# At most three of the late weight transfers on their way at a time

## The chip, the cores and the metric

The kernel runs on one core of one Trainium2 chip. The metric is the device time in microseconds (us) of one execution; the time of a kernel is the median of several. Five engines work side by side, each on its own queue of instructions: PE (TensorE, matrix products and transposes), DVE (VectorE), ACT (ScalarE), POOL (GpSimd) and SP (SyncE). SP computes nothing here. It issues nearly all DMA transfers, strictly in the order of its queue: an issue that has to wait holds up all issues behind it. A transfer's end is seen through a semaphore, and "landing" means the moment at which that semaphore says that all of its data are in place.

## The reference

Two layers stand one behind the other. First comes block-sparse attention over 4 batches, 8 heads, 768 positions and a head dimension of 64. Blocks of 32 positions attend to their neighbours, to the first and last block, and to three sampled blocks; the first and the last block attend to everything.

```
scores = scale * np.matmul(q, k.transpose(0, 1, 3, 2))
...
scores = np.where(mask, scores, -1000000000.0)
...
return np.matmul(attn, v).astype(np.float32)
```

Its output, 3072 rows of 512, is the input x of a soft mixture of experts with 8 experts and 4 slots each:

```
logits = x @ phi
d = softmax of logits over the 3072 rows;  slot_input = d.T @ x
h = np.maximum(slot_input[e] @ w1[e], 0.0);  slot_out[e] = h @ w2[e]
c = softmax of logits over the 32 slots;  out = c @ slot_out
```

Everything is in 32-bit floating point. The two weights w1 and w2 are 8 x 512 x 1024 and 8 x 1024 x 512, 33.6 MB in all, over half of the bytes that the kernel moves.

## The kernel before

**Stages.** The attention runs batch by batch over pairs of blocks. For each pair PE computes scores (`s`, L516), DVE and ACT make exponentials of them (L533, L538), DVE transposes them (L545), and PE multiplies them with the values (`av`, L610). POOL copies the three sampled blocks' values into staging tiles `vrs` (L461). Finished tiles of x are transposed (`mxt`, L803), turned into logits (`ml`) and summed into the slots' input (`ms`). After the last tile a short chain of small steps gives the slots' input `sT`. Then the feed-forward runs: sixteen steps `ffn1` (`pf`, L1227) with w1, sixteen steps `ffn2` (`pso`, L1235) with w2, eight for each half (`s_` = 0, 1) of the output's columns. The results of a half are combined with the softmax c (`po`, L1331), copied out (`ob`) and stored (L1288 to L1296).

**Weights.** The weights are cut into NW = 64 tiles of 128 x 1024 numbers, 512 KB each, used in the order of their numbers, two for each step. All loads go through `load_w` (L205, issue in L211) and `load_wk` (L230) onto SP's queue. There isn't room for all of them at once:

- Tiles 0 to 10 (pool `wpre`), 11 to 13 (`ktile`), 14 to 19 (`v0`) and 20 to 22 (`ptd`) are loaded during the attention, in pieces of 32 rows and 128 KB. The last three groups take the place of keys, values and probabilities that are no longer needed.
- Tiles 23 to 25 go into the second buffer of the keys as soon as it is free (the `("ktile", "k", 12, 13)` entry of L1038), each in two pieces of 512 columns, 256 KB. In the trace they are called `kw`.
- Tiles 26 to 43 are the late ones (`load_late`, L1180, called in L1210 to L1214): twelve go where the attention's staging tiles were (`w`), six into the values' second buffer (`v`), each again in two pieces of 256 KB, in the order of LORD (L59), in which a negative number means one of the six.
- Tiles 44 to 63 are loaded whole, 512 KB each, each when `done_w` (L1216) and `next_w` (L1193) find that an earlier tile's place has been used up.

**What sets the order.** Up to L1147 a planner (class `Plan`) lists all steps with costs and due times in a model of its own and emits them in that order; the pieces of tiles 0 to 22 are also paced (`pace`): each waits for a product that the planner expects to be done by then (L176 to L180), and their model keeps a rate. The pieces of tiles 23 to 25 belong to the plan too, without pacing. From L1153 on, the loads are emitted as the program writes them; what they wait for is that their place is free, and for the DMA semaphore that they share with an earlier transfer. The planner also emits small fill products on PE where it expects it to wait (`warm`, `st` in L376).

Of the kernel before, what the change touches and what calls it, by code (L numbers as in the profile page):

```python
# [21 lines left out]
P = 128  # L22
# [34 lines left out]


LORD = [0, 1, 2, 3, 4, 5, -1, -2, -3, -4, 6, 7, 8, 9, -5, -6, 10, 11]  # L59
LCOLS = [slice(c, c + LC) for c in range(0, WP, LC)]  # L60
H1, HALF = 3, 4
CPES = [0, 0, 3, 3, 3, 2, 0, 0]
# [14 lines left out]
class Plan:  # L77
# [6 lines left out]
    def add(self, f, opts, deps, key, acq=(), byte=0, pre=None, pace=False):  # L84
        t = Task(f, opts if isinstance(opts, list) else [opts], deps, key, acq, byte, pre, pace)
        self.tasks.append(t)
        return t
# [96 lines left out]
def attn_moe_kernel(ctx, tc, qT, kT, vfull, vtab, sampled, phi, w1, w2, out):  # L184
    nc = tc.nc
    PE, ACT, DVE, POOL, SP = nc.tensor, nc.scalar, nc.vector, nc.gpsimd, nc.sync
# [18 lines left out]
    def load_w(m, pool, t=None, rows=slice(0, P), cols=slice(0, WP)):  # L205
        if wtile[m] is None and t is None:
            t = pool.tile([P, WP], F32, name=f"w{m}", tag="w")
        elif t is None:
            t = wtile[m].rearrange("p c f -> p (c f)")
        n, j = m // PW, m % PW  # L210
        i = SP.dma_start(out=t[rows, cols], in_=wsrc[n].rearrange("p c f -> p (c f)")[rows, j * WP + cols.start:j * WP + cols.stop])  # L211
        wtile[m] = t.rearrange("p (c f) -> p c f", f=512 if n < 2 * NE else CW)
        return i

    wk = {}

    def new_wk(tag):
        k = KW[tag]
        if tag == "ktile":
            wk[tag] = pk.tile([P, k, WP], F32, name="kw", tag=tag)  # L220
        else:
            buf = ptdb if tag == "ptd" else vbuf[int(tag[1])]
            if tag == LATEW[1]:

                o = [VH * (j % 2) + WP * (j // 2) for j in range(k)]
                wk[tag] = [buf[:, c:c + WP] for c in o]
            else:
                wk[tag] = buf[:, 0:k * WP].rearrange("p (k f) -> p k f", k=k)

    def load_wk(m, tag, j, rows=slice(0, P), cols=slice(0, WP)):  # L230

        return load_w(m + j, None, wk[tag][j] if tag == LATEW[1] else wk[tag][:, j, :], rows, cols)
# [127 lines left out]
    add = plan.add  # L360
# [675 lines left out]
    m, n = NPRE, first[B - 1]  # L1036
    t_last = state.t_acc
    for tag, pool, n0, n1 in (("ktile", "k", 3, 5), ("v0", "v", 5, 10), ("ptd", "ptd", 5, 8), ("ktile", "k", 12, 13)):  # L1038
        go = lambda j: [qks[min(N - 1, n + n0 + (n1 - n0) * j // KW[tag])]]
        a_w = add(lambda t, tag=tag: new_wk(tag), ("NONE", 0.0), go(0), N + m, acq=[(pool, [t_last])])  # L1040
        for j in range(KW[tag]):
            parts = [(slice(r, r + LR), slice(0, WP)) for r in range(0, P, LR)]
            if n0 == 12:
                parts = [(slice(0, P), c) for c in LCOLS]
            for i, (r, c) in enumerate(parts):
                add(lambda t, m=m, tag=tag, j=j, r=r, c=c: load_wk(m, tag, j, r, c), ("SP", 0.47), go(j) + [a_w],
                    N + m + j + i / 4, byte=4 * WP * P // len(parts), pace=n0 < 12)
        m += KW[tag]

# [118 lines left out]
    wpool = [wpre] * NPRE  # L1168
# [11 lines left out]
    def load_late(pool, j=None):  # L1180

        m = len(wpool)
        for c in LCOLS:
            if j is None:
                load_w(m, pool, None, slice(0, P), c)
            else:
                load_wk(m - j, pool.tag, j, slice(0, P), c)
        wpool.append(pool)

    for tag in EARLYW:  # L1190
# [14 lines left out]
    load_group(LATEW[0], False)  # L1205

    new_wk(LATEW[1])
    lw, vw = [Place(lwb, f"w{n}") for n in range(NLB)], Group(LATEW[1])
    lw += [Place(pw, f"ptt{(nt[0] + r) % PTB}") for r in (2, 3)]
    for n in LORD:  # L1210
        if n < 0:
            load_late(vw, -1 - n)
        else:
            load_late(lw[n])  # L1214
# [214 lines left out]
```

## Time and profile before

| | |
|---|---|
| time, median of 3 | 316.43 us (315.21 to 322.23) |
| the profiled execution's own time | 316.63 us |
| its span, first to last instruction | 314.6 us |
| mean granted clock of TensorE in it | 0.984 |
| DMA packets, bytes | 34658, 63.62 MB |
| HBM read, written | 56.19 MB, 6.29 MB |

Groups of instructions in the profile have the line of the kernel, the engine, the operation, then what is written and read by the program's names (`av<-v,ptt`), shapes, and a count. PEld is the weight load of TensorE, which overlaps PE. A row of the chain of waits has the start, the length and the step, with what it is or what it waited for; "issue" is time in which an engine waited for nothing that the profile shows. A row of the timeline has the start, the length, the engine (SPq: issue on SP's queue), the line, the operation, the names and the count. A row of the DMA issues has the names, the queue, the count, the KB of each and the median time from issue to landing. A row of stretches has the stretch, its length, each engine's busy time and count, the granted TensorE clock, the DMA engines' busy share and the GB/s. The DMA digits of the page are tenths of the 16 DMA engines' time in 40 equal slices of the span.

### The profile page before, as it was taken

What the parts mean: (1) busy time and instruction counts of PE and PEld (TensorE: products, weight loads), DVE (VectorE), ACT (ScalarE), POOL (GpSimd) and SP (SyncE); (2) the same over time, 40 slices, a digit from 0 to 9 for tenths busy, and PEclk for the clock granted to TensorE, in tenths of its full rate; (3) what the DMA queues carried; (4) which work ended last, traced back from release to release, by engine and by line L of the source; (5) the groups of instructions that cost most, each with busy time, mean ns of one, the idle gap of its engine ahead of it and who ended that gap; (6) DMA issues with size and microseconds to landing.
All of it is one profiled execution on the core that took longest, in us unless ns stands there. A gap on an engine that the chain in (4) does not pass through costs nothing.

```text
span 314.6 us, 17616 instructions
## 1 busy us (share of the span) xinstructions
PE 281.6 (90%) x7167; PEld 193.2 (61%) x7167; DVE 215.2 (68%) x500; ACT 165.1 (52%) x509; POOL 180.5 (57%) x503
## 2 busy tenths in 40 slices
PE   7499799799999999999999999998995989999950
PEld 6148566466776666768577667865574764356640
DVE  4789876658998598888987878996895136012360
ACT  0856574853666877546867753675841051102450
POOL 2879498765856779685698966678656114000000
PEclk9999999999999999999999999999999899999995
DMA  7935778510276634034564420768789999999998
GB/s 246 400 110 174 212 215 222 152 40 3 58 195 188 176 93 128 5 105 121 182 187 131 114 71 21 200 180 231 212 226 319 334 346 367 409 407 408 327 301 272
DMA packets 34658, 63.62 MB, mean 202 GB/s; under 512 B 5649, under 2 KB 19090, under 8 KB 34578
## 3 DMA queue, kind: packets, MB, share of 16 engines
q1 hardware_dynamic: 34432, 62.37, 62.5%
q8 instruction: 56, 0.92, 1.3%
q14 instruction: 24, 0.20, 0.2%
q10 hardware_dynamic: 146, 0.13, 0.1%
HBM read 56.19 MB, written 6.29 MB: 199 GB/s over the span
## 4 chain that ended last, share of the span: by engine, by line
PE 65%; DMA 12%; DVE 5%; issue 4%; ACT 3%; POOL 2%; SPq 2%; POOLq 2%; ACTq 1%; DVEq 0%
PE av L610 26%; PE s L516 10%; DMA q<-in_qT_dram 8%; PE avd L610 6%; PE pf L1227 5%; PE pso L1235 4%; PE mxt L803 4%; PE sd L712 3%; DMA v<-in_vfull_dram 2%; DMA out_dram<-ob 2%; PE ms L888 2%; PE ml L838 2%; PE st L376 1%; ACT p L538 1%; ACTq L342 1%
## 5 line engine op out<-in xcount | busy, mean ns | idle before, releaser
L461 POOL COPY vrs<-v 128x260 f32 x264 | 95.6, 407 | 31.1 <-PE av L610 21.8
L538 ACT ACTIVATE p<-s,nm 128x256 f32<-128x256 f32 x176 | 72.3, 476 | 14.6 <-DVE nm L533 12.1
L610 PE MATMUL av<-v,ptt 64*64 64x130 f32 (+2 forms) x1728 | 75.0, 285 | 0.0
L545 DVE STREAM_TRANSPOSE ptt<-p 128x512 f32<-128x512 f32 x88 | 58.8, 693 | 19.0 <-ACT p L538 18.9
L610 PEld LDWEIGHTS av<-v,ptt 64*64 64x64 f32 (+2 forms) x1728 | 50.4, 132 | 27.0 <-issue 16.9
L516 PE MATMUL s<-kst,q 64*32 64x256 f32 x1408 | 53.8, 380 | 7.4 <-POOL kst L445 2.8
L533 DVE TENSOR_REDUCE nm<-s 128x2 f32<-128x512 f32 x88 | 55.3, 671 | 0.2
L610 PE MATMUL av<-vrs,ptt 64*32 64x130 f32 x2112 | 47.8, 275 | 5.8 <-issue 5.5
L437 POOL COPY kst<-ktile 128x384 f32<-128x384 f32 x88 | 42.9, 510 | 14.7 <-PE s L516 12.6
L443 ACT ACTIVATE kst<-ktile 128x128 f32 x174 | 39.6, 305 | 11.7 <-PE s L516 8.7
L516 PEld LDWEIGHTS s<-kst,q 64*32 64x32 f32 x1408 | 28.5, 106 | 21.6 <-ACT p L538 6.2
L610 PEld LDWEIGHTS av<-vrs,ptt 64*32 64x32 f32 x2112 | 35.7, 105 | 9.5 <-issue 8.6
L354 ACT COPY xT<-mxt 128x512 f32<-128x512 f32 (+1 forms) x21 | 11.9, 566 | 33.2 <-PE mxt L803 31.8
L610 PE MATMUL avd<-v,ptd 64*64 64x130 f32 x768 | 24.0, 271 | 0.9 <-DVE ptd L747 0.4
L743 ACT ACTIVATE pd<-sd,nb 128x384 f32<-128x384 f32 x32 | 16.6, 577 | 14.7 <-DVE nb L738 14.2
L610 PEld LDWEIGHTS avd<-v,ptd 64*64 64x64 f32 x768 | 22.1, 132 | 2.8 <-PE s L516 1.5
L445 POOL COPY kst<-ktile 128x128 f32 x90 | 22.6, 297 | 1.0 <-issue 0.4
L478 ACT ACTIVATE q<-q 128x256 f32<-128x256 f32 x26 | 10.8, 419 | 16.8 <-DMA q<-in_qT_dram 15.6
L803 PE MATMUL mxt<-ident,x 128*128 128x128 f32 x96 | 16.4, 292 | 3.5 <-DVE x L605 2.3
L803 PEld LDWEIGHTS mxt<-ident,x 128*128 128x128 f32 x96 | 10.6, 144 | 14.1 <-DVE x L605 5.0
L712 PE MATMUL sd<-ktile,q 64*32 64x384 f32 x256 | 16.6, 496 | 1.2 <-ACT p L538 1.2
L730 DVE TENSOR_REDUCE nm<-sd 128x1 f32<-128x384 f32 x32 | 16.2, 542 | 2.1 <-PE sd L712 2.0
(119 smaller groups left out, 277.1 us busy)
## 6 DMA issues: line engine op xcount, KB each, us to landing
w<-in_w_dram SPq DMA_DIRECT2D x24, 256.0 KB, 5.6
q<-in_qT_dram SPq DMA_DIRECT2D x47, 128.0 KB, 2.8
w<-in_w_dram SPq DMA_DIRECT2D x44, 128.0 KB, 3.4
w<-in_w_dram SPq DMA_DIRECT2D x11, 512.0 KB, 9.6
out_dram<-ob SPq DMA_DIRECT2D x22, 256.0 KB, 3.2
ktile<-in_kT_dram SPq DMA_DIRECT2D x48, 96.0 KB, 3.3
v<-in_w_dram SPq DMA_DIRECT2D x24, 128.0 KB, 3.4
v<-in_w_dram SPq DMA_DIRECT2D x12, 256.0 KB, 5.9
```

The source lines that it names most:

```text
L437: POOL.tensor_copy(out=st[:, :, w:w + 96], in_=kv[:, :, (i - 1) * BLK:(i + 2) * BLK])
L443: ACT.activation(out=st[:, :, o:o + BLK], in_=src, func=AF.Copy, scale=1.0)
L445: POOL.tensor_copy(out=st[:, :, o:o + BLK], in_=src)
L461: POOL.tensor_copy(out=st[:, :, j:j + 1, :], in_=vf[:, :, ds(t.vals[j], 1), :])
L516: PE.matmul(u.s[r][32 * p:32 * p + 32, j, :], lhsT=u.q[s_, p, j, :], rhs=kd[j][0][s_, p, :], start=True, stop=True)
L533: DVE.tensor_reduce(out=u.nm[r], in_=u.s[r], axis=AX.X, op=ALU.max, negate=True)
L538: ACT.activation(out=u.p[r][:, j, :], in_=u.s[r][:, j, :], func=AF.Exp, bias=u.nm[r][:, j:j + 1], scale=1.0)
L545: DVE.transpose(out=T.pt[r][:, :, 2 * w:2 * w + 2, :].rearrange("p k j q -> p j k q"), in_=u.p[r].rearrange("p j (k q) -> p j k q", k=8))
L610: PE.matmul(av[:, r * 2 * D1:(r + 1) * 2 * D1].rearrange("p (a d) -> p a d", a=2), lhsT=lhsT, rhs=rhs, start=start, stop=stop)
L712: PE.matmul(u.s[r][k][32 * p:32 * p + 32, :], lhsT=T.dq.q[s_, p, j, :], rhs=kt[s_, p, 384 * k:384 * (k + 1)], start=True, stop=True)
L743: ACT.activation(out=u.p[r][k], in_=u.s[r][k], func=AF.Exp, bias=u.nb[r], scale=1.0)
L803: PE.transpose(T.px[:, c, :], T.x[:, c * P:(c + 1) * P], ident)
```

## The change

A list `late` keeps the names of issues. `few(i)` adds issue i to that list and, from the fourth on, makes i wait until the transfer three places in front of it in the list has landed. It is called for the pieces of tiles 23 to 25 (six pieces) and for the first ten tiles of the late loop (twenty pieces): MLATE is the number of tiles placed at the loop's start plus ten. The last eight late tiles, and the reloads behind them, have no such wait of their own, but stand behind the others on SP's queue. What is loaded, from where to where, in which pieces and in which order the program writes it, stays the same.

```
+NLATE = 3
...
+    late = []
+
+    def few(i):
+
+        if len(late) >= NLATE:
+            tc.add_manual_dep(i.ins, late[-NLATE], mybir.DependencyInfo(
+                mybir.DependencyClass.Sync, mybir.DependencyReason.DATA), reason="pace")
+        late.append(i.ins.name)
...
-                add(lambda t, m=m, tag=tag, j=j, r=r, c=c: load_wk(m, tag, j, r, c), ("SP", 0.47), go(j) + [a_w],
+                def load(t, m=m, tag=tag, j=j, r=r, c=c, last=n0 == 12):
+                    i = load_wk(m, tag, j, r, c)
+                    if last:
+                        few(i)
+                    return i
+                add(load, ("SP", 0.47), go(j) + [a_w],
                     N + m + j + i / 4, byte=4 * WP * P // len(parts), pace=n0 < 12)
...
         for c in LCOLS:
-            if j is None:
-                load_w(m, pool, None, slice(0, P), c)
-            else:
-                load_wk(m - j, pool.tag, j, slice(0, P), c)
+            i = load_w(m, pool, None, slice(0, P), c) if j is None else load_wk(m - j, pool.tag, j, slice(0, P), c)
+            if m < MLATE:
+                few(i)
...
     new_wk(LATEW[1])
+
+    MLATE = len(wpool) + 10
```

## The prediction

> **What bounds the kernel now.** I read the page first, then the chain of waits of the last quarter, then the stretches of that quarter with their DMA rates, and last the issues of SP (SyncE, whose queue issues the weight loads) with their times to landing. Span 314.6 us; the profiled execution took 316.63 us, so 2.03 us lie around the span.
>
> ```profile
> PE 281.6 (90%) x7167; PEld 193.2 (61%) x7167; DVE 215.2 (68%) x500; ACT 165.1 (52%) x509; POOL 180.5 (57%) x503
> DMA  7935778510276634034564420768789999999998
> ```
>
> PE is busy for 90% of the span, but the DMA digits stand at 9 over the last quarter too, so two things can set the end there. The chain from 234 us on shows what PE does in the stretch that the change touches:
>
> ```profile
> 234.09 4.71 PE av L610 x172
> 238.79 3.54 issue
> 242.33 0.41 PE av L610 x4
> 242.74 2.32 PE st L376 x12
> 245.91 5.24 PE av L610 x166
> 261.95 1.06 PE pf L1227 x7
> ```
>
> The attention's last products but one (av) stop four matmuls before their end, for 3.54 us, and the chain names no releaser ("issue"). Nothing that PE needs is late: it had run 172 matmuls of the same group. What fits is PE's own code. The DMA view lists q8, "instruction"; of two equal stretches of 8 us, 225 to 233 and 234 to 242, its rows are, in this order:
>
> ```profile
> q8 instruction: 2, 0.03, 1.6%
> ...
> q8 instruction: 1, 0.02, 1.6%
> ```
>
> A share of 1.6% of 16 engines over 8 us is 2.05 us: about 1.02 us for each of two packets before, 2.05 us for the single one beside the stall. So a code packet took twice as long just there. After the stall the clock falls:
>
> ```profile
> 232.00:242.00 10.00, 6.79 (x218) 4.93 (x209) 7.08 (x20) 2.16 (x5) 7.75 (x22) 1.00 0.89 269
> 242.00:257.00 15.00, 13.21 (x243) 10.80 (x243) 3.47 (x17) 3.68 (x12) 2.84 (x7) 0.89 0.99 347
> 243.00:246.00 3.00, 3.00 (x18) 2.67 (x16) 1.15 (x4) 0.05 (x1) 0.87 (x2) 0.55 1.01 361
> 246.00:249.00 3.00, 3.00 (x90) 2.50 (x92) 0.00 (x0) 0.54 (x1) 0.00 (x0) 0.88 1.00 341
> 263.00:295.00 32.00, 32.00 (x388) 15.72 (x382) 7.63 (x24) 5.79 (x12) 3.59 (x6) 1.00 1.02 395
> ```
>
> The last three columns are granted clock, DMA share and GB/s. Granted 0.55 and 0.88 cost 3 x 0.45 + 3 x 0.12 = 1.7 us of PE work. From 263 to 295 us PE is busy 32.00 of 32.00 us while DMA moves 395 GB/s: PE computes and the queue delivers, both without a gap. Which of them ends last is read from the final pieces:
>
> ```profile
> 283.36 1.63 SPq L211 DMA_DIRECT2D w<-in_w_dram  x2
> w<-in_w_dram SPq DMA_DIRECT2D x1, 512.0 KB, 10.4
> 284.66 0.33 SPq L211 DMA_DIRECT2D w<-in_w_dram  x1
> 296.90 1.05 PE L1235 MATMUL pso<-w,hT 128*32 128x256 f32 x16
> ```
>
> The last weight tile is issued at 284.66, lands 10.4 us later, at 295.06, and PE comes to the last pair at 296.90. The weight stream has 1.84 us of slack against PE, no more. That number decides this case: whatever PE wins before, the last product can come only 1.84 us earlier unless the stream is earlier too, and whatever the stream loses above 1.84 us is added to the time.
>
> **What the change adds.** No transfer, byte or arithmetic is added or removed. 26 issues of 256 KB are counted by the new list: six kw pieces, twelve w, eight v; from the fourth on each gets one wait, 23 in all. They are these, with the first pieces behind them that stay as they are, and, singly, the first and the last landing:
>
> ```profile
> 232.18 3.86 SPq L211 DMA_DIRECT2D kw<-in_w_dram  x6
> 236.08 10.21 SPq L211 DMA_DIRECT2D w<-in_w_dram  x12
> 246.39 5.08 SPq L211 DMA_DIRECT2D v<-in_w_dram  x8
> 251.87 5.57 SPq L211 DMA_DIRECT2D w<-in_w_dram  x8
> kw<-in_w_dram SPq DMA_DIRECT2D x1, 256.0 KB, 4.4
> 251.14 0.33 SPq L211 DMA_DIRECT2D v<-in_w_dram  x1
> v<-in_w_dram SPq DMA_DIRECT2D x1, 256.0 KB, 6.0
> ```
>
> So the first lands at 232.18 + 4.4 = 236.6 and the 26th at 251.14 + 6.0 = 257.1. By then a landing takes 6.0 us at a piece every 5.08 / 8 = 0.64 us: eight or nine pieces are on the way, and the change makes that three.
>
> **The price of the wait.** With three on the way, three pieces pass in the time that one takes from issue to landing, L, and a step of some 0.05 us (an estimate: the page's chain has gaps of that size between a release and its follower). Pieces 1 to 3 go out as before; the second lands about 0.6 us behind the first, at 237.2. The 26th is eight rounds behind the second: it lands at 237.2 + 8 x (L + 0.05). The trace has no 256 KB load with so few beside it, so L comes from 128 KB loads with none to three on the way, whose rows are (from 184.8, 111.4 and 135.8 us on):
>
> ```profile
> w<-in_w_dram SPq DMA_DIRECT2D x4, 128.0 KB, 2.5
> v<-in_vtab_dram SPq DMA_DIRECT2D x2, 113.8 KB, 2.2
> q<-in_qT_dram SPq DMA_DIRECT2D x1, 128.0 KB, 2.0
> w<-in_w_dram SPq DMA_DIRECT2D x3, 128.0 KB, 3.7
> ```
>
> The missing 128 KB (for the v row 142 KB) at 395 GB/s add 0.33 us (0.37). L then lies between 2.0 + 0.33 = 2.33 and 3.7 + 0.33 = 4.03 us. I take 2.85 (the same weights, 2.5 + 0.33) for the two rounds up to about 243 us, where DVE and POOL are still busy for 7 of 10 us, and 2.2 + 0.37 = 2.57, the v row, for the six rounds behind, where they are busy for 3 of 15. Sum: 2 x 2.90 + 6 x 2.62 = 21.5 us, the 26th lands at 258.7, 1.6 us later than now. With 2.33 throughout it lands at 256.2, 0.9 us earlier; with 4.03 at 269.8, 12.7 us later.
>
> Queued behind the waiting issues on SP is all that comes later: sixteen late pieces without the new wait, twenty reloads of 512 KB, and the stores. In the present run the loads take from 257.1 to 295.06 us, 38.0 us, at the rate of the stretch row above; DMA has nothing to catch up with, so I let the 1.6 us reach the last tile whole: 296.7. No product between is near it. The paced pieces are tiles for the second half of the feed-forward, after 273 us:
>
> ```profile
> 273.34 0.60 PE L1227 MATMUL pf<-kw,sT 128*32 128x512 f32 x2
> 275.04 2.76 PE L1227 MATMUL pf<-w,sT 128*32 128x512 f32 x24
> ```
>
> The wait itself thus costs nothing where it stands; its cover against the first users is over ten us, and what it uses up is the 1.84 us at the very end.
>
> **What PE can win.** If the code packet comes in time, 3.54 us of stall and 1.7 us of low clock go. The next thing that is late is POOL, whose copies of the sampled values the last av needs:
>
> ```profile
> 239.12 2.22 POOL L461 COPY vrs<-v 128x260 f32 x6
> 245.84 1.99 PE L610 MATMUL av<-v,ptt 64*128 64x130 f32 x30
> ```
>
> They end at 241.34 and the last av begins at 245.84 now, so 4.5 us can be won there, and 0.36 us of the clock behind it: 4.9 us at most, 1.5% of the time. On the other side nothing is won. I take about 3.5 us; in the sum it doesn't count, since after it PE reaches the last pair at 293.4 and waits for the tile until 296.7.
>
> The Trainium skill, page "DMA: Bandwidth & Descriptors", section "Queues, rings and completion order", speaks against that gain: a DMA engine takes turns between its queues by packets of some 9 to 17 descriptors, so code would not stand behind everything that is queued. The stretch from 263 to 295 us, with 512 KB pieces landing after some 10 us and no gap in PE, agrees with that; the doubled packet beside the stall doesn't. The same page ("Rules for kernel authors") asks for 1 MiB or more per transfer for full bandwidth, while three pieces here are 768 KB.
>
> **The sum.** End = last tile's landing, 1.6 us later, less the slack of 1.84: 0.2 us earlier than 314.6, span 314.4, time 316.4 us. The median shown, 316.43 us, is 0.2 below the profiled execution, so I carry no correction: **316.4 us**.
>
> **Rivals.**
>
> *The stall stays.* The code packet is late for another cause, or PE's use of code simply meets one slow packet. For it, the code queue's row for 263 to 295 us:
>
> ```profile
> q8 instruction: 3, 0.05, 0.6%
> ```
>
> That is 3.07 us for three packets, 1.02 us each, beside a queue that is as full as it gets. Then PE comes to the last pair at 296.9 as now and a stream 1.6 us late is still in time: 316.6 us. It decides as long as the stream's delay stays below 1.84 us. Chance 0.25. The rule of the Trainium skill on taking turns, named above, would give this case.
>
> *The stream gains with PE.* With fewer pieces on the way each lands in 2.33 us, the stream is 0.9 us early, and PE's 3.5 us count up to 1.84 + 0.9 = 2.7: 313.9 us. If the stream were earlier by 3 us, all 4.9 of PE: 311.7. For it: 269 GB/s from 232 to 242 us with six or more on the way, so depth buys no rate there. Against it: three times 256 KB per 2.38 us is 330 GB/s, below the 347 of the stretch behind. Chance 0.17.
>
> *The queue runs dry (slower).* At each landing SP must wake and start a transfer afresh, and landings stay as slow as the 3.7 us row. Place: the 23 waits; price: 8 x 0.05 + 8 x L against the 19.9 us from 237.2 to 257.1. The time passes 2% (6.3 us) when the stream is 6.3 + 1.84 = 8.1 us late, at L = 3.45. With L = 3.5 it is 8.5 us late and the time 323.3 us. For it: that row, and 3.7 to 4.6 us for kw pieces now; against it: three rows of four. Chance 0.10.
>
> *The change doesn't hold.* The late loads after the planned part are not in an order written by hand, so pieces without a wait could be issued in front of waiting ones and fill the queue: 316.6 us. Chance 0.03.
>
> **How the numbers follow.** The forecast has 0.45, its own range 314.7 (no delay, all slack won) to 319 (4.1 us late, L about 2.95 throughout). The range reaches from 311.7, PE's whole gain, to 321.0, L = 3.2 throughout (8 x 3.25 = 26.0, landing 263.2, 6.1 us late, 4.3 us on the time). About 2% is what a measurement of this kernel tells from no change. Faster by more needs 6.3 us, over the 4.9 that PE can win: 0.04 is left for what I don't see. Slower by more is the third rival, 0.10. Within: 0.86.
>
> **What would show it.** SP: 23 waits of L211 on its own DMA between 232 and 258 us, and kw, w and v pieces of 256 KB landing in 2.3 to 3 us in place of 4.5 to 6.6. PE: no idle time of 3 us with "issue" near 239 us, and clock 1.00 from 243 us. The end: PE idle before the last pso products with the DMA of w or v named as releaser, as the sign that the stream sets the time; the last weight landing at 296 to 297 us. I am wrong if landings of the paced pieces stay above 3.4 us, if the stall is there with three pieces on the way, or if the stream makes up its delay behind 258 us.

## The result, and the profile after

The changed kernel takes 335.46 us (median of 4, 334.85 to 336.47) against 317.19 us for the kernel before on the same chip (median of 4, 315.21 to 322.23): 18.3 us slower by the medians, 1.061 times the time, interval 1.056 to 1.067. A ratio and its interval, here and below, leave out executions over 1.5% above the fastest of the same kernel, while a median is over all of them, so a ratio need not be the quotient of two medians. The prediction was 316.4 us, no change. In later executions (the last experiment) the ratio was 1.052.

The profiled execution took 334.85 us with a span of 333.1 us. The kernel's lines have moved: issues of weights are now L212, `av` is L620, `pso` L1251. From the page, the DMA digits (one slice is 333.1 / 40 = 8.3 us):

```profile
DMA  7925757600375451154645116787807799999998
```

The digits no longer stand at 9 from the 31st slice on: there is a 0 in the 30th (241.5 to 249.8 us), and two slices at 7 behind it. The hole is seen on SP's timeline (start, length, queue, line, operation, names, count):

```profile
236.89 2.08 SPq L212 DMA_DIRECT2D kw<-in_w_dram  x3
250.47 0.33 SPq L212 DMA_DIRECT2D w<-in_w_dram  x1
250.90 1.33 SPq L212 DMA_DIRECT2D kw<-in_w_dram  x3
```

Before, six kw pieces went out without a break. Now three go, then nothing for 11.5 us, then one `w` piece, and then the other three. That one is the first piece of tile 36. It isn't in the list `late`; it is the first of the sixteen late pieces that the change leaves without a wait of their own, and the eleventh tile in LORD's order. In the program's text it stands behind the 26 paced ones. In the executed queue it is the fourth issue, and it goes on like this: after every three paced pieces comes one unpaced (the run with this order written out, below, repeats the picture). Its place in SBUF is one that the last av products still read, as SP's waits show (238 to 252 us: line, waited for, us in total, times, longest):

```profile
SPq L212 <- PE av L620: 11.4, 1, 11.4
```

Everything behind it on SP waits too. Three stretches (PE, PEld, DVE, ACT, POOL busy; then clock, DMA share, GB/s) show the hole, the paced part behind it, and the end:

```profile
238.00:250.40 12.40, 12.30 (x364) 9.79 (x364) 7.58 (x22) 2.74 (x6) 8.17 (x22) 1.00 0.24 71
250.40:263.00 12.60, 10.76 (x113) 7.65 (x111) 6.24 (x29) 5.55 (x18) 0.99 (x2) 1.00 0.72 233
280.00:315.00 35.00, 25.83 (x266) 11.06 (x262) 4.43 (x11) 5.26 (x11) 0.00 (x0) 0.95 1.02 391
```

For 12.4 us DMA moves 71 GB/s. For the next 12.6 us it moves 233, where the kernel before moved 347. At the end the queue is full and the rate is 391, as before; but PE, then busy for 32.00 of 32.00 us, is now busy for 25.83 of 35.00. The chain of waits (start, length, step) says what PE waits for:

```profile
238.75 4.83 PE av L620 x175
243.58 1.54 PE st L386 x12
245.76 4.66 PE av L620 x161
251.37 4.00 DMA kw<-in_w_dram
255.36 0.02 issue
255.38 3.51 DMA w<-in_w_dram
...
292.06 10.17 DMA kw<-in_w_dram
...
304.85 10.13 DMA w<-in_w_dram
```

Before 251 us the chain goes through PE, and the 3.54 us of "issue" between the av groups are gone. From 251.37 us to the last weight landing at 304.85 + 10.13 = 314.98 us it goes mostly through weight loads. And the last products, on PE's timeline, wait for them:

```profile
313.77 0.64 PE L1251 MATMUL pso<-w,hT 128*32 128x256 f32 x8 [0.63 <-DMA w<-in_w_dram]
315.03 0.64 PE L1251 MATMUL pso<-w,hT 128*32 128x256 f32 x8 [0.62 <-DMA w<-in_w_dram]
```

The last landing is 314.98 - 295.06 = 19.9 us later than before; less the 1.84 us of slack this makes 18.1 us, and the span grew by 18.5. But the first kw issue already stood 236.89 - 232.18 = 4.7 us later, for reasons ahead of the change's first place. So the profiles are compared from the first kw issue on: from there to the last landing it was 295.06 - 232.18 = 62.9 us before and is 78.1 after.

### The profile page after: what moved, and what is told of

Its sections match the earlier page's. It is cut to its first block, busy times and chain, and to the rows that moved or that the text cites. A ratio compares the mean times of both kernels' runs of the same rounds, so it can differ in the third digit from the quotient of the medians.

```text
span 333.1 us, 17615 instructions
## 1 busy us (share of the span) xinstructions
PE 289.2 (87%) x7167; PEld 193.3 (58%) x7167; DVE 215.4 (65%) x500; ACT 165.1 (50%) x509; POOL 181.1 (54%) x503
## 4 chain that ended last, share of the span: by engine, by line
PE 42%; DMA 31%; DVE 8%; issue 4%; POOLq 4%; POOL 4%; SPq 2%; ACT 2%; ACTq 1%
PE av L620 22%; DMA w<-in_w_dram 10%; PE s L526 6%; DMA q<-in_qT_dram 6%; PE avd L620 5%; DMA kw<-in_w_dram 4%; DMA v<-in_w_dram 4%; POOLq L352 3%; PE sd L722 3%; PE mxt L813 2%; POOL vrs L471 2%; DMA phis<-in_phi_dram 2%; DMA out_dram<-ob 2%; DMA v<-in_vfull_dram 2%; DVE x L615 2%
## 5 line engine op out<-in xcount | busy, mean ns | idle before, releaser
L620 PE MATMUL av<-v,ptt 64*64 64x130 f32 (+2 forms) x1728 | 75.8, 288 | 0.0
L620 PEld LDWEIGHTS av<-v,ptt 64*64 64x64 f32 (+2 forms) x1728 | 50.8, 133 | 27.3 <-issue 18.0
L526 PE MATMUL s<-kst,q 64*32 64x256 f32 x1408 | 54.7, 391 | 11.3 <-ACT p L548 4.9
L620 PE MATMUL av<-vrs,ptt 64*32 64x130 f32 x2112 | 45.8, 278 | 1.3 <-issue 1.3
L453 ACT ACTIVATE kst<-ktile 128x128 f32 x174 | 39.5, 305 | 11.5 <-PE s L526 8.7
L620 PEld LDWEIGHTS av<-vrs,ptt 64*32 64x32 f32 x2112 | 36.1, 106 | 2.5 <-issue 2.2
L620 PE MATMUL avd<-v,ptd 64*64 64x130 f32 x768 | 23.7, 271 | 1.0 <-DVE ptd L757 0.7
L620 PEld LDWEIGHTS avd<-v,ptd 64*64 64x64 f32 x768 | 22.0, 132 | 3.2 <-PE s L526 1.5
L488 ACT ACTIVATE q<-q 128x256 f32<-128x256 f32 x26 | 10.8, 417 | 19.2 <-DMA q<-in_qT_dram 16.7
L722 PE MATMUL sd<-ktile,q 64*32 64x384 f32 x256 | 17.5, 506 | 1.0 <-ACT p L548 0.6
```

The lines of the kernel that those rows point to most:

```text
L453: ACT.activation(out=st[:, :, o:o + BLK], in_=src, func=AF.Copy, scale=1.0)
L526: PE.matmul(u.s[r][32 * p:32 * p + 32, j, :], lhsT=u.q[s_, p, j, :], rhs=kd[j][0][s_, p, :], start=True, stop=True)
L620: PE.matmul(av[:, r * 2 * D1:(r + 1) * 2 * D1].rearrange("p (a d) -> p a d", a=2), lhsT=lhsT, rhs=rhs, start=start, stop=stop)
L722: PE.matmul(u.s[r][k][32 * p:32 * p + 32, :], lhsT=T.dq.q[s_, p, j, :], rhs=kt[s_, p, 384 * k:384 * (k + 1)], start=True, stop=True)
```

## The experiments

Two things changed at once: the order of SP's queue and the waits. The first theory was that the order (SP standing at tile 36) accounts for the loss. The rival was that three transfers on the way are by themselves too few. Between DMA and PE there was a second question: does PE's stall follow the number of bytes or pieces on the way, or has it another cause?

In the kernel before and in the changed one, SP's instructions behind the plan are put in order by a list scheduler; those of PE, DVE, ACT and POOL stand as the program writes them. The set that says which engines are written by hand is `MAN`. All runs below but the last, which is the changed kernel itself, add SP to it:

```
-MAN = {E_.PE, E_.DVE, E_.Activation, E_.Pool}
+MAN = {E_.PE, E_.DVE, E_.Activation, E_.Pool, E_.SP}
```

But for the third run, which writes out another order, SP's order is then that of the kernel before.

**The order held, no waits.** Beside `MAN`: `NLATE = 99`, so no issue waits.

> SP's issues are kept in the order in which the program writes them, with no wait between late pieces: the instructions of every engine are those of the kernel before. A control, and a second profile of it. All theories: 316 to 318 us, last weight tile landed at 295 us. If the PE stall of 3.5 us near 239 us was an accident of one execution it is gone here; if it belongs to the full queue it is here again.

Measured 316.11 us against 315.36, ratio 1.003 (0.999 to 1.008). SP's order written out costs nothing that shows, and PE's stall is there, 2.12 us where the kernel before had 3.54; for the stall this run is the control (PE's timeline; in brackets the idle time in front):

```profile
243.89 0.42 PE L620 MATMUL av<-vrs,ptt 64*32 64x130 f32 x4 [2.12 <-issue]
```

**The order held, the waits as in the change.** `MAN` alone, NLATE = 3.

> The 23 waits of the change, SP's issues kept in the order of the kernel before. Theory A (the order did half of it, the waits the other half): no wait of SP for the last av product; landings of 3.3 to 4.0 us as in the changed kernel from 254 us on, so eight rounds of 3.4 to 4.0 us in place of the 2.6 to 2.9 predicted, the stream 7 to 12 us late, 1.84 us of it absorbed: 322 to 327 us. Theory B (the waits alone are the loss, the order is harmless): 335 us as in the changed kernel. The prediction's own sum: 316.4 us.

Measured 327.72 us, ratio 1.043 (1.038 to 1.047): 12.4 us slower with the waits alone, just above the 322 to 327 us of theory A. SP's timeline, SP's waits from 230 to 262 us, the issues from 234.3 to 261.3 us (names, count, KB, median us to landing), and the end of the chain:

```profile
230.59 6.06 SPq L212 DMA_DIRECT2D kw<-in_w_dram  x6
237.90 13.63 SPq L212 DMA_DIRECT2D w<-in_w_dram  x12
252.39 8.91 SPq L212 DMA_DIRECT2D v<-in_w_dram  x8
```

```profile
SPq L212 <- DMA w<-in_w_dram: 11.3, 12, 2.9
SPq L212 <- DMA kw<-in_w_dram: 4.0, 6, 1.4
SPq L212 <- DMA v<-in_w_dram: 3.3, 5, 1.0
```

```profile
w<-in_w_dram SPq DMA_DIRECT2D x12, 256.0 KB, 4.3
v<-in_w_dram SPq DMA_DIRECT2D x8, 256.0 KB, 3.3
kw<-in_w_dram SPq DMA_DIRECT2D x3, 256.0 KB, 3.3
```

```profile
294.76 10.10 DMA w<-in_w_dram
```

The order is that of before, and SP's waits are now 23, all on its own DMA, 18.6 us in sum. Three on the way land in (12 x 4.3 + 8 x 3.3 + 3 x 3.3) / 23 = 3.8 us (a mean of the medians), where the forecast had 2.57 to 2.85. The last landing comes at 304.86, 74.3 us behind the first kw issue and 11.4 us later than before. PE's stall is gone, and the feed-forward (`pf`) starts earlier (PE's timeline):

```profile
237.68 0.41 PE L620 MATMUL av<-vrs,ptt 64*32 64x130 f32 x4 [0.39 <-issue]
...
255.69 4.92 PE L1243 MATMUL pf<-w,sT 128*32 128x512 f32 x42 [0.38 <-ACT sT L364]
```

**After's order, no waits.** SP's issues are emitted by hand in the order in which the changed kernel executed them, and none waits for an earlier transfer:

```
+        late.append(i)
+        if len(late) <= 3:
+            i()
...
+            (late if m < MLATE else free).append(i)
...
+    todo_, free_ = late[3:], list(free)
+    while todo_ or free_:
+        if len(free_) > 8:
+            free_.pop(0)()
+        elif not todo_:
+            free_.pop(0)()
+        for i in range(3):
+            if todo_:
+                todo_.pop(0)()
```

> SP's issues in exactly the order of the changed kernel (tile 36's first piece between the third and the fourth kw piece, and so on), without any of the 23 waits. Theory A: SP stands at that piece for some 11 us until the last av product is done, then the queue is full at once; the stream has 79 pieces of 256 KB to bring at 0.66 us each from about 250 us on, last landing near 304 us, 9 us late, 7 us over the kernel before: 322 to 326 us. Theory B: the order is harmless, 316 to 318 us.

Measured 323.75 us, ratio 1.030 (1.023 to 1.037): 8.4 us slower with the order alone. SP's wait from 229 to 246 us, its timeline, and the end of the chain:

```profile
SPq L212 <- PE av L619: 13.7, 1, 13.7
```

```profile
229.62 1.32 SPq L212 DMA_DIRECT2D kw<-in_w_dram  x3
244.71 0.33 SPq L212 DMA_DIRECT2D w<-in_w_dram  x1
```

```profile
292.71 10.20 DMA w<-in_w_dram
```

The stream ends at 302.91, 73.3 us behind the first kw issue, 10.4 us later than before; less the slack of 1.84 that is 8.6 us. So the first theory and its rival both hold: either alone costs more than 2%. Their sum is 8.4 + 12.4 = 20.8 us, and the change cost 18.3. That the sum isn't reached fits two things, which were not tried apart: while SP stands, the pieces that it waits for land anyway, and the unpaced pieces between the paced ones make four on the way in place of three.

**Five on the way.** `NLATE = 5`.

> Five on the way in place of three, order of the kernel before kept. Theory A: landings of about 4.2 us, so a piece every 0.85 us against 0.80 now; the stream 0 to 3 us late, 1.84 us of it absorbed, and PE's stall near 239 us gone or shorter: 315 to 318 us. Theory B (any wait between late pieces is a loss): 325 us or more.

Measured 318.65 us, ratio 1.016 (1.009 to 1.022): slightly above theory A, which also had the stall shorter or gone. The stall is back, and the stream is still 3.0 us late (287.17 + 10.10 - 231.39 = 65.9 us; issues from 233 to 256 us, PE, and SP's timeline and chain):

```profile
w<-in_w_dram SPq DMA_DIRECT2D x16, 256.0 KB, 4.8
```

```profile
240.87 0.51 PE L620 MATMUL av<-vrs,ptt 64*32 64x130 f32 x4 [2.94 <-issue]
```

```profile
231.39 4.77 SPq L212 DMA_DIRECT2D kw<-in_w_dram  x6
```

```profile
287.17 10.10 DMA w<-in_w_dram
```

With five pieces the kernel has the worse of both.

**Only the first ten pieces paced.** PE is done with av by the time that the later pieces go out, so their waits can't help it. `MLATE = len(wpool) + 2`: six kw and four w pieces, three on the way.

> Three on the way for the first ten late pieces only (six kw, four w), order of the kernel before kept, all others without the wait. With the waits on 26 pieces and the order kept, the ninth piece landed 12.7 us after the first kw issue, against 12.5 us in the kernel before: up to there the waits had cost nothing, and PE's stall was gone. Theory A (the loss grows with the number of paced pieces, the gain is had in the first ten): last weight landing 62 to 64 us after the first kw issue, no PE idle time of 2 us or more around 239 us, time 0.99 to 1.00 of the kernel before. Theory B (each wait costs its share of the 12 us): 10 of 26, so 4.8 us: 320 us, ratio 1.015.

Measured 323.12 us against 318.11, ratio 1.022 (1.014 to 1.029). The stall is nearly gone, the stream ends at 292.15 + 11.65 = 303.80, or 67.0 us behind the first kw issue at 236.84, 4.1 us late, and PE waits for v in the last steps (PE's timeline; chain of waits):

```profile
243.98 0.42 PE L620 MATMUL av<-vrs,ptt 64*32 64x130 f32 x4 [0.52 <-issue]
296.22 0.64 PE L1251 MATMUL pso<-v,hT 128*32 128x256 f32 x8 [2.00 <-DMA v<-in_w_dram]
```

```profile
292.15 11.65 DMA w<-in_w_dram
```

Theory A, that seven waits would be cheap enough for PE's gain to show, is refuted. B's ratio of 1.015 lies within the interval.

**512 KB pieces, three on the way.** `LCOLS = [slice(0, WP)]`, so each late tile is one transfer, and twice the bytes are on the way. It also leaves 13 paced pieces with 10 waits in place of 26 with 23.

> Late tiles loaded whole, 512 KB a piece, three on the way, order of the kernel before kept: 1.5 MB on the way in place of 0.75. Theory A (bytes on the way set both the rate and the stall): landings of 4.5 to 5.5 us, a piece every 1.5 to 1.8 us against two of 0.8 now, so a stream about as long as in the kernel before, PE's stall of 2 to 3.5 us back: 315 to 319 us. Theory B (the count of three sets the rate, whatever the size, because every third landing is waited for): 325 us and no stall.

Measured 318.94 us against 318.11, ratio 1.012 (1.007 to 1.016), where theory A had it; B's 325 us is refuted. The stall is 1.30 us (row below, first), less than A's 2 to 3.5, and the landings are longer than A's 4.5 to 5.5: the issues from 240 to 266 us have 7.9 us for w and 6.4 for v, unpaced ones included.

**512 KB pieces, no waits.** The same with `NLATE = 99`.

> Late tiles loaded whole, 512 KB a piece, no waits, order kept: up to 4 MB on the way. If the depth of the queue is what makes PE's code late, PE's stall near 239 us is longer than the 2.1 to 3.5 us with 256 KB pieces: 4 us or more. The stream can only gain (landing of the last weight 60 to 63 us after the first kw issue), but PE then sets the end: 315 to 319 us.

Measured 317.95 us against 318.11, ratio 1.008 (1.003 to 1.013). PE's stall, first with three and then with the full queue of 512 KB pieces (the second in the longest of its ten executions, 320.36 us):

```profile
244.82 0.41 PE L620 MATMUL av<-vrs,ptt 64*32 64x130 f32 x4 [1.30 <-issue]
```

```profile
246.45 0.41 PE L620 MATMUL av<-vrs,ptt 64*32 64x130 f32 x4 [2.43 <-issue]
```

A stall of 4 us or more was expected, if bytes on the way made it; it is no longer than the 2.12 us with 256 KB pieces. So a deeper queue doesn't make the stall longer than a full queue of small pieces does.

**Ten paced, then 512 KB.** The first ten as above, the rest whole.

> As with the waits on the first ten pieces of 256 KB, and the late tiles behind them loaded whole, 512 KB a piece, without waits. Theory A: stall gone as with ten waits, and a deeper queue behind keeps the DMA engines fuller while PE's code is fetched, so the stream is 1 to 3 us shorter: 0.985 to 0.995 of the kernel before. Rival: the deeper queue makes PE's next code packet late, near 251 us, and gives the gain back: ratio 1.0.

Measured 319.11 us against 318.11, ratio 1.011 (1.005 to 1.017). Theory A, a gain, is refuted; the ratio is a little above the rival's 1.0. The stall is not gone, although all late pieces issued up to there were paced ones of 256 KB (PE's timeline; the profiled execution, 325.30 us, is the longest of its six):

```profile
246.73 0.41 PE L620 MATMUL av<-vrs,ptt 64*32 64x130 f32 x4 [1.35 <-issue]
```

None of these eight versions beats the kernel before. With three small pieces on the way the stall was 0.39, 0.52 and 1.35 us in three runs, with three large ones 1.30, with five small ones or a full queue 2.12 to 3.54. Three and a full queue are told apart by this; three small and three large are not. The 1.35 us stand in a run in which the code packet of the next paragraph starts 2.2 us behind the first kw issue, while the last pieces ahead of kw (`ptd`) are still on the way; in the other two it starts 4.4 us behind it.

**What PE waits for in the stall.** The forecast argued that it is PE's own code. The traces bear it out. The DMA view, taken in windows of 0.2 us, gives the start of each packet of the queue q8 ("instruction"), and its share gives the length. In all nine profiles with idle time at this place, PE goes on 1.4 to 1.5 us after the end of such a packet:

| run | PE idle | q8 packet starts, takes | packet before it starts | PE goes on |
|---|---|---|---|---|
| kernel before | 3.54 | 238.9, 2.0 | 232.6 | 242.33 |
| order held, no waits | 2.12 | 241.3, 1.2 | 235.5 | 243.89 |
| five on the way | 2.94 | 238.5, 1.0 | 232.1 | 240.87 |
| 512 KB, no waits | 2.43 | 243.9, 1.1 | 238.0 | 246.45 |
| 512 KB, three | 1.30 | 242.3, 1.1 | 237.5 | 244.82 |
| ten paced, then 512 KB | 1.35 | 243.1, 2.1 | 239.4 | 246.73 |
| after's order, no waits | 0.75 | 234.7, 1.5 | 231.1 | 237.61 |
| ten paced | 0.52 | 241.3, 1.2 | 237.3 | 243.98 |
| order held, three | 0.39 | 235.0, 1.3 | 230.9 | 237.68 |

The packet took twice as long only in two of them. In the control, in the run with five and in that with 512 KB and no waits it took its usual 1.0 to 1.2 us but started 5.8 to 6.4 us behind the one before it, where it is 3.7 to 4.1 in the three runs with the shortest stalls. The doubled packet that the forecast read is shown first, of 238 to 240 us, and the control's, of 240 to 242 us, second:

```profile
q8 instruction: 1, 0.02, 6.3%
...
q8 instruction: 1, 0.02, 3.7%
```

So with a full queue the code is late, mostly because its packet starts late. Why it starts late the traces don't show.

**One and two on the way.** `NLATE = 1` and `NLATE = 2`, one execution each, for the time of a landing by itself.

> One late piece on the way at a time, order kept: every landing of 256 KB is seen alone. Theory A (the prediction's rows were right for a piece alone, and what it missed is that three pieces queue behind each other and behind PE's code): landings of 2.3 to 2.9 us where no code packet of PE is on the way, 1 us or more longer where one is; 26 pieces in some 70 us, time 350 to 365 us. Theory B (a 256 KB piece takes longer than the 128 KB rows plus bytes let expect, whatever is beside it): landings of 3.3 us or more without a code packet, 370 us or more.

> Two on the way, order kept. Theory A: landings between those of one and of three on the way (3.8 us mean with three), about 3.0 us, so 1.5 us a piece, 26 pieces in some 40 us, 330 to 335 us. Theory B: landings of 3.5 us or more, 1.8 us a piece, 340 us or more.

Measured 372.26 and 339.77 us (before: 319.94, one execution). Both times lie above theory A's and nearer B's, but the landings without a code packet are A's. With one on the way: a piece at 276.2 us, one at 272.2 us, and the code packet of PE (queue q8) that passes from 273 to 274.6 us beside the second:

```profile
w<-in_w_dram SPq DMA_DIRECT2D x1, 256.0 KB, 2.6
...
w<-in_w_dram SPq DMA_DIRECT2D x1, 256.0 KB, 4.0
...
q8 instruction: 1, 0.02, 5.3%
...
v<-in_w_dram SPq DMA_DIRECT2D x8, 256.0 KB, 2.7
```

The last row is that of v from 284.2 to 312 us. With two on the way, 262.2 to 278 us:

```profile
v<-in_w_dram SPq DMA_DIRECT2D x8, 256.0 KB, 3.0
```

And with three on the way, four pieces from 246.5 us on with no code packet, and three from 241.8 us on of which a code packet of PE passes:

```profile
w<-in_w_dram SPq DMA_DIRECT2D x4, 256.0 KB, 3.1
...
w<-in_w_dram SPq DMA_DIRECT2D x3, 256.0 KB, 4.6
```

So a lone piece mostly lands in 2.6 to 2.7 us, and the forecast's L of 2.57 to 2.85 is right for that case: but it was written for three on the way. Four more lone pieces, the first four kw ones from 236.1 us on, have a code packet beside them each, and land in 3.9 to 4.8 us.

**The changed kernel once more.** Unchanged, for the 4.7 us that were lost ahead of the first kw issue.

> The changed kernel, unchanged, in further executions. Its profiled execution came to the first kw issue at 236.9 us, 4.7 us later than the profiled execution of the kernel before (232.2), although nothing in front of that place is changed by the text of the change. Theory A (chance: such leads and lags differ from execution to execution, as between 229.6 and 240.9 us in the other runs' profiles): the first kw issue stands somewhere else, near 230 to 234 us, and the span behind it is 96.2 us as before; the time is then 327 to 331 us, 1.035 to 1.05 of the kernel before. Theory B (the changed kernel is slower ahead of that place as well): the first kw issue is again at 236 us or later, and the time 333 us or more, 1.055 or more. Both expect SP to stand for 11 to 14 us at the first piece of tile 36.

Measured 333.88 us against 315.67 (median of 7), ratio 1.052 (1.039 to 1.065). Its profiled execution took 335.03 us, span 333.2. SP's timeline and SP's wait:

```profile
232.45 1.30 SPq L212 DMA_DIRECT2D kw<-in_w_dram  x3
248.08 0.33 SPq L212 DMA_DIRECT2D w<-in_w_dram  x1
```

```profile
SPq L212 <- PE av L620: 14.3, 1, 14.3
```

Neither theory holds whole. The first kw issue stands at 232.45 us, where it was before, so the 4.7 us were that execution's own, as A says. But the span behind it is 333.2 - 232.45 = 100.8 us, not 96.2: SP stands for 14.3 us in place of 11.4, and the stream behind the block takes longer too. This is the longest of the four executions, which took 329.13 to 335.03 us, and the ratio of 1.052 goes by the two shorter ones. So how much of the 18.3 us is the change's own is known only roughly: 13.8 us behind the first kw issue in the first profile (96.2 against 82.4 before), and 18.3 in this one. Why the part behind that issue differs by some 4.5 us between two executions stays open.

## Why the prediction was wrong

Two steps failed: the order of SP's queue, and the size of the term L. Each alone puts the time outside the forecast.

**"All that comes later" stands behind the waits: wrong.** The sum let SP's queue run in the order of the text. The rival "the change doesn't hold" did say that unpaced pieces could be issued in front of waiting ones, and that is what happened, but it priced this at nothing (they "fill the queue", 316.6 us) and had a chance of 0.03. The missing step was to ask of the piece that comes forward what it itself waits for. Tile 36's place is free only after the last av, so the piece fills nothing: it blocks the queue, for 11.4 us, and by the run with this order alone that costs 8.4 us. The text of the kernel named both halves: that SP's order behind the plan is not written by hand, and that each place has its user. The kernel before, with the same scheduler and no waits, has the written order, and so has the run with the waits and SP's order held; so it was the two together that moved the pieces. How the scheduler weighs a wait stays open.

**The price of the wait, L = 2.57 to 2.85 us: mis-sized.** Three on the way land in 3.8 us. The formula was right: 5.0 us to the second landing and 8 x (3.8 + 0.05) = 30.8 give 35.8 us from the first kw issue to the 26th landing, and in the run the 26th piece, issued 0.33 us before its group ends at 252.39 + 8.91 = 261.30, lands 5.3 us later, 35.7 us behind the first kw issue (before: 257.1 - 232.18 = 24.9). That they agree to 0.1 us is in part luck: this last landing, with unpaced pieces behind it, is longer than the mean, and the rounds before it were shorter. What failed is the choice of rows. The forecast took 128 KB loads with "none to three" on the way as if they were three, added the bytes at full rate, and so had the time of a lone piece, which the later run measured at 2.6 to 2.7. The 3.7 us row, which it named as the upper bound and weighed at one of four, was nearest. By the forecast's own bound, 2% lost at L = 3.45, the slower rival "the queue runs dry" was the case: with 3.8 it gives 35.8 - 24.9 - 1.84 = 9.1 us on the time, and the waits alone cost 12.4 by the medians (10.3 by the profiles from the first kw issue on: 323.3 - 230.59 against 314.6 - 232.18). The rival's reason was not what was seen: SP doesn't lose its time in waking up, since in the chain of the changed kernel 0.02 us lie between a landing and the transfer behind it; the landings are slow.

**Slack of 1.84 us at the end: right, and it decided.** Compared from the first kw issue on, profile against profile, the span follows the last landing less the slack: order alone 10.4 - 1.84 = 8.6 against 9.3 us, waits alone 9.6 against 10.3, five on the way 1.2 against 1.8, ten paced 2.2 against 2.0, the change 13.4 against 13.8. By the medians the order alone fits this too (8.4). Others cost more than it gives: the waits alone 12.4 in place of 9.6, and ten paced, by the ratio of 1.022, some 7 us in place of 2.2; where that comes from stays open. PE idles before the last pso products with DMA as releaser, the sign that was named for a stream that sets the end.

**PE's stall goes with three on the way: right in the main.** It was 3.54 us, 2.12 in the control, and is 0.39 with the order held; in one of the three runs that had three small pieces on the way there, 1.35 us were left. That the packet of code takes twice as long was right for the profile shown, but is not the rule: mostly it starts late. PE reaches the feed-forward's first product 25.1 us behind the first kw issue in that run (255.69 - 230.59), where it was 261.95 - 232.18 = 29.8: 4.7 us won, within the 4.9 at most. Against the control, 263.51 - 234.69 = 28.8, it is 3.7 us, close to the 3.5 that the forecast took. In the stretch rows of after the clock stays at 1.00 where it had been 0.89. The gain shows nowhere in the time, as the sum had it. The Trainium skill ("DMA: Bandwidth & Descriptors", section "Queues, rings and completion order") lets an engine take turns between its queues, by which the stall wouldn't depend on what is queued; the runs with three, five and a full queue of 256 KB pieces disagree (0.39, 2.94, 2.12 us, with the order held), while the one with a full queue of 512 KB pieces, 2.43 us, agrees that more bytes behind add nothing.

**"DMA has nothing to catch up with": right.** The late stream stayed late to the last tile: 10.8 us at the 26th landing and 11.4 at the last, with the waits alone.

## What to carry to other kernels

A wait put on one transfer is a wait put on its queue, and on an engine whose order a scheduler sets, it is also a new order: work out which instructions may now come forward and what those wait for themselves, or write that engine's order by hand. Where a stream of loads runs without a gap to the end of the kernel, its rate is the time: a limit on what is on the way is priced by measured landings with just so many on the way, not by those of lone loads. Where the stream sets the end, a stall on another engine that the limit removes is worth at most the slack between the two.

## What the runs showed of the hardware

The more 256 KB loads were on the way, the later each of them landed, already while the DMA engines were far from full: 2.7 us alone, 3.0 with two, 3.1 with three where no code packet passed and 3.8 over all, 4.8 with five (the step from two to three, 0.1 us, is the smallest). Alone and two at a time they move 95 and 167 GB/s at a share of 0.29 and 0.49 (stretches of 284.2 to 312 and 262.2 to 278 us in their runs), three at a time some 208 to 228, where the full queue of the kernel before moves 347 to 395.

```profile
232.00:245.00 13.00, 12.39 (x364) 9.70 (x364) 7.30 (x23) 2.74 (x6) 8.19 (x22) 1.00 0.68 228
245.00:261.00 16.00, 14.37 (x143) 8.81 (x147) 8.33 (x37) 5.55 (x18) 4.31 (x8) 1.00 0.62 208
```

These are the stretches of the run with the waits alone, three on the way: a share of 0.62 to 0.68. Why the landings stretch with the engines a third idle is open. The coupling between code and data goes both ways. The stall follows the end of PE's code packet by 1.4 to 1.5 us, and with five pieces or a full queue on the way it was 2.1 to 3.5 us. In return, the lone piece that took 4.0 us in place of 2.6 had a code packet beside it of 5.3% of 1.6 us, which over 16 engines is 1.36 us. Where each piece waits for an earlier landing, such a delay passes on to all pieces behind it.
